# Three of 32 V stores issued as row scatters, with eight of their rows moved to the SyncE queue

## The chip, the cores and the metric

The kernel runs on one core of one Trainium2 chip. The metric is device time in microseconds (us) from one launch to its end; three runs of the kernel before gave 736.78, 735.42 and 736.70, with a median of 736.7 us. Engine names are those of the profile: PE multiplies matrices, DVE and ACT work on vectors, POOL is GpSimd, and SP is SyncE, which only issues transfers here. All transfers, whichever engine issues them, are carried out by the core's 16 DMA engines.

## The reference, cut to what matters

One decoding step of attention (32 heads, a cache of 8192 keys and values of width 128 for each head) is added to a gated MLP, and the function returns the output and the gradients of all its inputs.

```
q = (xn @ wq).reshape(B, 1, 32, 128)                  # xn: layernorm of x
p = softmax(einsum("bhqd,bhkd->bhqk", q, k_cache) * Dh**-0.5)
o = einsum("bhqk,bhkd->bhqd", p, v_cache)
out = x + o.reshape(B, 1, 4096) @ wo + swiglu(xn; w1, w3, w2)
outputs: out, d x, d k_cache, d v_cache, d wq, d wo, d w1, d w3, d w2
```

For each head the gradients of the two caches are outer products, d V = p x (d o) and d K = (d s) x q, as large as the caches: 2 MB of bf16 for each of K and V of each head. So the kernel reads 151 MB, writes 151 MB and computes little.

## The kernel before, in words

**Slots.** A head's K or V is one tile of 128 partitions x 8192 values: 16,384 bytes in each partition, 2 MB in all. There are ten such slots (kv0 to kv9). Four of them first hold the MLP's weights. A slot's life is: loaded with K or V of a head, read by PE, overwritten in place by DVE with the gradient (`outer`, L460 to L471, two instructions of half a tile), stored, loaded again. Ahead, V of head h is called Vh and its store likewise.

**Queues.** Every K and V load is issued by SP through `fifo` (L104), strictly in order: V0, K1, V1 and so on as slots come free. `store` (L473) issues the gradient's store from POOL, puts the slot back on the list and calls `load_next` (L120), which gives the next load to SP; that load waits for the store's landing. POOL also issues the stores of d wo (L505, 640 KB for a group of four heads) and d wq (L514, 640 KB), and the loads of a group's wq and wo (L111, L113). An instruction that waits holds up all that stands behind it on its engine; POOL and SP are such queues.

**Order.** The order of instructions is written out by hand (`manual_schedule`, L72). In `head(h)` (L729), DVE first finishes V of head h-1 (`outers_a`, whose `store("V", h-1)` issues Vh-1) and half of K, and in the middle of the head the rest of K (`outers_b`, store of K). In a head whose number is a multiple of four, `fin_wo` then issues d wo of the group before. So around V8 POOL's order is V7, K7, d wo, **V8**, K8, V9, d wq, K9, V10, K10; around V16 and V24 it is the same with 8 or 16 added. The MLP (L538) stands ahead of head 2.

**DMA waits.** DMAs take eight semaphores in turn on POOL and eight on SP, so each also waits for the landing of the one eight before it on its own engine. Besides that a store of V or K waits for DVE's outer product. No store waits for another store's data: their rows in DRAM are apart.

**A store as packets.** A store of a tile is 128 packets of 16,384 bytes, eight for each of the 16 DMA engines. Each engine adds one to the store's semaphore when its own eight have landed; the store has landed at the sixteenth.

## Time and profile before

| | |
|---|---|
| median of three runs | 736.7 us |
| the profiled execution's own time | 735.86 us |
| its span, first to last instruction | 734.1 us |
| transferred | 303.52 MB, mean 413 GB/s |
| busy share of the span: PE, DVE, ACT, POOL | 82%, 63%, 51%, 9% |
| store of a tile, issue to landing (median) | 45.2 us |
| load of K, of V, issue to landing (median) | 18.7, 22.3 us |
| one issue of a store on POOL, of a load on SP | 0.53, 0.33 us |

The page's part 1 gives busy times, part 2 the span in 40 slices with the DMA engines' busy share as one digit, part 3 the transfers by queue: q0 holds what POOL issues, q1 what SP issues, q8 and q14 are fetches of instructions. Part 6 gives, for each kind of transfer, its median time from issue to landing. Waits of SP's and POOL's queues have a view of their own, and the windows view gives the busy share of the DMA engines in chosen stretches: 1.00 is all sixteen, 0.06 is one of them.

### The profile page before, as it was taken

To read this page: it belongs to the slowest core of one execution; us is meant where nothing else is said; L and a number is where in the kernel's file an instruction comes from. 1 tells how busy PE (TensorE), PEld (TensorE's weight loads), DVE (VectorE), ACT (ScalarE), POOL (GpSimd) and SP (SyncE) were. 2 spreads that over 40 slices of the span, in tenths; PEclk is the share of its full clock that TensorE was granted. 3 is DMA by queue.
4 is the path that set the end of the run, shared out by engine and by line. 5 is a ranking of instruction groups with operands and counts; after the bars stand their busy time and mean duration, and the time that the engine had idled before them with its cause. 6 is when DMAs were issued, how large, how long until landed. Compare 5 with 4: busy or idle time off the path is not lost.

```text
span 734.1 us, 13013 instructions
## 1 busy us (share of the span) xinstructions
PE 601.6 (82%) x5186; PEld 374.7 (51%) x5193; DVE 460.3 (63%) x811; ACT 375.5 (51%) x727; POOL 64.7 (9%) x109
## 2 busy tenths in 40 slices
PE   4988589999899899988897869878798797886920
PEld 2556466665565566544554545544464454554510
DVE  4279637687867776767475555667367674664780
ACT  3641646655666666654454446544465453554500
POOL 0110100001011100200010100201002000001010
PEclk9996799999999999999899989999899998998955
DMA  8999999999999999999999999999999999999991
GB/s 351 402 413 419 426 425 419 430 429 430 427 429 421 427 426 427 423 427 425 428 429 413 427 427 423 422 428 428 428 427 413 427 426 429 428 420 430 423 410 79
DMA packets 27134, 303.52 MB, mean 413 GB/s; under 512 B 2798, under 2 KB 4146, under 8 KB 10434
## 3 DMA queue, kind: packets, MB, share of 16 engines
q0 software_dynamic: 14944, 160.52, 52.0%
q1 hardware_dynamic: 12126, 142.17, 46.0%
q8 instruction: 41, 0.67, 0.3%
q14 instruction: 19, 0.16, 0.1%
q10 hardware_dynamic: 4, 0.00, 0.0%
HBM read 151.34 MB, written 151.34 MB: 412 GB/s over the span
## 4 chain that ended last, share of the span: by engine, by line
DMA 30%; PE 28%; issue 17%; another core or an unknown queue 11%; DVE 7%; ACT 3%; POOL 1%; SPq 0%; POOLq 0%; ACTq 0%; DVEq 0%
DMA wo_g<-in_A_wo_dram 16%; PE pT L314 13%; DMA out_dram<-kv 8%; DMA kv<-in_A_k_cache_dram 4%; PE sA L335 4%; PE X L429 2%; PE dA L335 2%; DMA kv<-in_A_v_cache_dram 2%; DVE kv L462 2%; PE m L352 1%; ACT kv L624 1%; DVE side L253 1%; PE gu_ps L543 1%; PE dh_ps L554 1%
## 5 line engine op out<-in xcount | busy, mean ns | idle before, releaser
L316 ACT COPY KT<-pT 128x512 f32<-128x512 f32 x512 | 288.0, 588 | 231.0 <-PE pT L314 211.8
L314 PE MATMUL pT<-ident_f,kv 128*128 128x128 f32 x2048 | 304.6, 287 | 52.1 <-DMA kv<-in_A_k_cache_dram 34.5
L314 PEld LDWEIGHTS pT<-ident_f,kv 128*128 128x128 f32 x2048 | 234.2, 147 | 144.0 <-PE pT L314 52.1
L462 DVE TENSOR_TENSOR kv<-qd,U 128x4096 bf16<-128x4096 bf16 x64 | 146.0, 2283 | 0.0
L462 DVE TENSOR_TENSOR kv<-qd,P 128x4096 bf16<-128x4096 bf16 x64 | 143.6, 2284 | 0.0
L429 PE MATMUL X<-kv,Z 128*32 128x512 bf16 x1024 | 97.4, 414 | 1.4 <-DVE Z L446 1.4
L335 PE MATMUL dA<-KT,qz 128*32 128x512 bf16 x512 | 83.7, 406 | 0.0
L335 PE MATMUL sA<-KT,qz 128*32 128x512 bf16 x512 | 82.4, 401 | 0.0
L477 POOL DMA_DIRECT2D out_dram<-kv x64 | 34.7, 543 | 393.6 <-DVE kv L462 184.7
L412 DVE SCALAR_TENSOR_TENSOR U<-m,P 128x64 bf16<-128x64 f32 x32 | 7.4, 232 | 86.0 <-PE m L352 86.0
L429 PEld LDWEIGHTS <-Z 128*32 128x32 bf16 x1024 | 33.2, 101 | 35.1 <-issue 8.9
L335 PEld LDWEIGHTS <-qz 128*32 128x32 bf16 x1024 | 29.5, 95 | 40.4 <-issue 37.8
L378 DVE TENSOR_REDUCE mrow<-m 128x1 f32<-128x64 f32 x32 | 7.2, 224 | 56.1 <-PE m L352 56.0
L352 PE MATMUL m<-selc,KT 64*128 64x64 f32 x256 | 30.8, 244 | 11.7 <-ACT KT L342 11.7
L352 PEld LDWEIGHTS m<-selc,KT 64*128 64x128 f32 x256 | 21.8, 146 | 34.0 <-ACT KT L342 24.5
L253 DVE SCALAR_TENSOR_TENSOR side<-wo_g,g_bc 128x640 bf16<-128x640 bf16 x32 | 26.2, 820 | 16.6 <-DMA wo_g<-in_A_wo_dram 16.2
L372 ACT CAST qd<-pT 128x256 bf16<-128x256 f32 x32 | 11.9, 373 | 39.5 <-DVE kv L462 30.8
L385 DVE TENSOR_REDUCE negM<-m 128x1 f32<-128x128 f32 x32 | 9.3, 291 | 32.9 <-PE m L382 32.9
L510 DVE SCALAR_TENSOR_TENSOR wq_g<-wq_g,side 128x512 bf16<-128x512 bf16 x40 | 27.3, 682 | 0.0
L444 DVE SCALAR_TENSOR_TENSOR U<-m,P 128x128 bf16<-128x128 f32 x32 | 11.4, 356 | 15.4 <-PE m L442 15.4
L402 DVE RECIPROCAL rZ<-m 128x1 f32<-128x1 f32 x32 | 5.3, 166 | 24.2 <-PE m L396 24.2
L342 ACT COPY KT<-dA 64x512 f32<-64x512 f32 x32 | 18.6, 583 | 3.4 <-PE dA L335 3.4
(162 smaller groups left out, 392.1 us busy)
## 6 DMA issues: line engine op xcount, KB each, us to landing
out_dram<-kv POOLq DMA_DIRECT2D x64, 2048.0 KB, 45.2
kv<-in_A_k_cache_dram SPq DMA_DIRECT2D x32, 2048.0 KB, 18.7
kv<-in_A_v_cache_dram SPq DMA_DIRECT2D x32, 2048.0 KB, 22.3
out_dram<-wo_g POOLq DMA_DIRECT2D x8, 640.0 KB, 51.0
out_dram<-wq_g POOLq DMA_DIRECT2D x8, 640.0 KB, 48.6
wq_g<-in_A_wq_dram POOLq DMA_DIRECT2D x7, 640.0 KB, 30.8
wo_g<-in_A_wo_dram POOLq DMA_DIRECT2D x7, 640.0 KB, 34.9
kv<-in_B_w_dram SPq DMA_DIRECT2D x2, 1728.0 KB
```

Source lines behind the costliest of these rows:

```text
L253: nc.vector.scalar_tensor_tensor(junk[:], G_["wo"][:, hh, :], 1.0, g_bc[:], ALU.mult, ALU.mult, accum_out=G_["do"][:, hh:hh + 1])
L314: nc.tensor.transpose(pT[:, k * P:(k + 1) * P], W3[:, 4 * c + k, :], ident_f[:])
L316: nc.scalar.copy(KT[:].rearrange("p k w -> p (k w)"), pT[:])
L335: nc.tensor.matmul(S_[kind][q:q + QW, :], lhsT=S_["qz"][:, o:o + QW], rhs=KTb[c][:, par, :], start=(c0 == 0 and par == 0), stop=(c0 == NCH ...
L342: nc.scalar.copy(XS[0:QH].rearrange("p k w -> p (k w)"), S_.pop(kind)[0:QH, :])
L352: nc.tensor.matmul(S_["m"][:, b0:b0 + 4 * J].rearrange("p (x c k t) -> p k x c t", x=4, k=4, t=2)[:, k], lhsT=XS[0:QH, k, :], rhs=selc[0:Q ...
L372: nc.scalar.copy(qd[:].rearrange("p a d -> p (a d)"), hd[h].pop("ps_r"))
L429: nc.tensor.matmul(xg["X"][q:q + QW, :], lhsT=Z[:, o:o + QW], rhs=W[:, N4 * i:N4 * (i + 1)], start=(slot == 0 and i < 4), stop=(slot == NS ...
L444: nc.vector.scalar_tensor_tensor(S_["U2"][:], S_["V"][:, 0:J].unsqueeze(2).to_broadcast([P, J, 2]), S_["m"][:, OC + NS:OC + NS + 1], S_["P ...
L462: nc.vector.tensor_tensor(dst[:, lo * DH:hi * DH].rearrange("p (j a b) -> p j a b", a=DH // 2, b=2), vec.rearrange("p (a b) -> p a b", b=2 ...
L477: nc.gpsimd.dma_start((dkc if kind == "K" else dvc)[h], t[:])
L510: nc.vector.scalar_tensor_tensor(wq_g[:, ci, :], wq_g[:, ci, :], 1.0, dqb, ALU.mult, ALU.mult, accum_out=dxa[:, ci, g:g + 1])
```

## The change

For heads 8, 16 and 24 the V store is issued as an indirect DMA (a row scatter): a list of 128 row numbers says to which row of the output each partition's 16,384 bytes go. For partitions 16 to 19 and 48 to 51 the list holds a number beyond the bound (2 to the 20th is added), so that these eight rows are left out; SP then stores them in two transfers of four partitions each. The list is built once, at the start, by one iota on POOL and seven small instructions on DVE, from the identity matrix that is there already.

```
+    ROW_HEADS = (8, 16, 24)
+    SPARE = (16, 48)
+    dv_rows = out_3.rearrange("b h (p j) d -> (b h p) (j d)", p=P)
+    row_ix = consts.tile([P, 4], mybir.dt.uint32, name="row_ix")
+    row_i = consts.tile([P, 4], mybir.dt.int32, name="row_i")
+    nc.gpsimd.iota(row_i[:], [[8 * P, 4]], base=8 * P, channel_multiplier=1)
+    row_f = consts.tile([P, 4], F32, name="row_f")
+    nc.vector.tensor_copy(row_f[:], row_i[:])
+    skip = consts.tile([P, 2], F32, name="skip")
+    for n, lo in enumerate(SPARE):
+        nc.vector.tensor_reduce(skip[:, n:n + 1], ident_f[:, lo:lo + 4], AX.X, ALU.add)
+    nc.vector.tensor_tensor(skip[:, 0:1], skip[:, 0:1], skip[:, 1:2], ALU.add)
+    nc.vector.tensor_scalar(skip[:, 0:1], skip[:, 0:1], float(2 ** 20), None, ALU.mult)
+    nc.vector.tensor_scalar(row_f[:], row_f[:], skip[:, 0:1], None, ALU.add)
+    nc.vector.tensor_copy(row_ix[:], row_f[:])
...
-        nc.gpsimd.dma_start((dkc if kind == "K" else dvc)[h], t[:])
+        if kind == "V" and h in ROW_HEADS:
+            n = ROW_HEADS.index(h)
+            nc.gpsimd.indirect_dma_start(dv_rows, bass.IndirectOffsetOnAxis(ap=row_ix[:, n:n + 1], axis=0), t[:], None,
+                                         bounds_check=H * P - 1, oob_is_err=False)
+            for lo in SPARE:
+                fifo(dvc[h][lo:lo + 4], t[lo:lo + 4])
+        else:
+            nc.gpsimd.dma_start((dkc if kind == "K" else dvc)[h], t[:])
```

What the built program makes of it: a scatter's destination is the whole V output, since its rows are known only at run time. So the scatter of V8 waits for the landing of V7 (as well as for its outer product), V9 waits for the landing of the scatter, and so does SP's first four-row transfer; the load that takes the slot next waits for both four-row transfers. V16 and V24 wait in the same way. K8, which stands between V8 and V9 on POOL, has no such wait. Nothing else changes its place on any engine.

## The prediction

> **What bounds the kernel now.** I read the page's transfers first, then SP's waits, then the windows over the end of the span.

> ```profile
> span 734.1 us, 13013 instructions
> ...
> GB/s 351 402 413 419 426 425 419 430 429 430 427 429 421 427 426 427 423 427 425 428 429 413 427 427 423 422 428 428 428 427 413 427 426 429 428 420 430 423 410 79
> ...
> q0 software_dynamic: 14944, 160.52, 52.0%
> q1 hardware_dynamic: 12126, 142.17, 46.0%
> q8 instruction: 41, 0.67, 0.3%
> ```

> The rate is flat at 420 to 430 GB/s from the fourth slice to the last but two, and the queues' packets fill 98% of 16 engines' span: DMA is the bound, and no arithmetic engine is (PE 82%). The last slice falls to 79 GB/s. [...]

> ```profile
> SPq L105 <- DMA out_dram<-kv: 605.0, 58, 22.2
> ```

> SP waits 605 us for stores to land: a load starts when a store frees its slot, never for want of being asked. Now the end:

> ```profile
> 712.00:714.00 2.00, 0.56 (x2) 0.50 (x2) 1.22 (x8) 0.00 (x0) 0.87 (x1) 0.50 1.02 420
> ...
> 718.00:720.00 2.00, 0.00 (x0) 0.00 (x0) 0.00 (x0) 0.00 (x0) 0.00 (x0) 0.50 0.46 188
> 720.00:722.00 2.00, 0.00 (x0) 0.00 (x0) 0.00 (x0) 0.00 (x0) 0.00 (x0) 0.50 0.20 81
> 722.00:724.00 2.00, 0.00 (x0) 0.00 (x0) 0.00 (x0) 0.00 (x0) 0.00 (x0) 0.50 0.12 50
> 724.00:726.00 2.00, 0.00 (x0) 0.00 (x0) 0.00 (x0) 0.00 (x0) 0.00 (x0) 0.50 0.06 25
> 726.00:728.00 2.00, 0.00 (x0) 0.00 (x0) 0.00 (x0) 0.00 (x0) 0.00 (x0) 0.50 0.06 24
> 728.00:730.00 2.00, 0.00 (x0) 0.00 (x0) 0.00 (x0) 0.00 (x0) 0.00 (x0) 0.50 0.07 27
> 730.00:732.00 2.00, 0.00 (x0) 0.00 (x0) 0.00 (x0) 0.00 (x0) 0.00 (x0) 0.50 0.02 6
> ```

> The column before the last is the DMA engines' busy share. At 712 all sixteen work; by 722 two are left (0.12), and from 724 to 730 the share is 0.06, one sixteenth: **one DMA engine finishes alone, some 6.4 us after the fifteenth**. The sixteen increments of the last store's semaphore (d wq) say it more closely: half by 719.91, the fifteenth at 724.58, the sixteenth at 731.02. The lag grew: on V7's store the last was 0.7 us behind the fifteenth (248.38), on V16's 11.6 (444.41), on V24's 15.1 (617.19). Which engine it is the trace does not name. But the last q8 packet ends at 702.60, the next packet on that engine (it begins 15 ns before, as at other q8 packets) opens a gapless run of 71 packets, and that run is the one that ends last. [...]

> **The change, part by part.**

> *Removed.* Three scatters leave out 8 rows each: 24 packets of 16,384 bytes. Such a packet takes 611 ns, and the next on its engine starts 4 ns before its end: 24 x 0.607 = 14.6 us less for whatever engine had them. That all eight rows are one engine's share I cannot read in the trace. [...] Bounds for the late engine: all eight rows are its own, 14.6 us; four are, 7.3; none, 0. I take the first. Either of the first two ends it before the fifteenth, and then the fifteenth is the end: **gain 731.02 - 724.58 = 6.4 us**, not 14.6.

> *Added on other engines.* The eight rows go in six transfers of four rows. The only four-row transfer now is of fin_bf; its packets run on four engines which end all work at 716.5 to 719.7. If the new ones take the same four, each gains 6 x 0.607 = 3.6 us and ends by 723.4, before 724.58: cost 0.

> *First added wait: the scatter for the V store before it.* V8 was issued at 228.45 and may now go only when V7 has landed, 248.38: 20 us later. For V16 it is 391.13 to 422.92, for V24 562.88 to 595.69. Queued behind it on POOL stand K8, V9, d wq; none of them is needed by DVE or PE, only by SP, for slots. What matters is that no engine that sets the end runs out of packets. The late engine still holds K7 and d wo when V7 lands: they land at 254.72 and 261.21, so its cover is 12.8 us (12.8 at V16 and V24 too). Needed is the time from an issue to a first packet; the first POOL transfer, issued at 33.98, had its first packet at 38.23: 4.25 us. Engines that are ahead do run dry (the first is through d wo at 416.96, 6 us before V15's landing), but they have 5 to 15 us to spare at the end. Cost 0.

> *Second added wait: V9 for the scatter's landing.* In between stands K8 alone, and on the last engine it lands 6.5, 5.8 and 5.7 us after V8, V16 and V24 (276.48 - 269.99 and so on). Against 4.25 us this cover holds, though barely; on the fifteenth engine it is 4.8, 9.7 and 9.8. I take 0.2 us for each scatter. Bounds: 0, and 4.25 us a wait if there is no cover.

> *Third: SP.* The first four-row transfer waits for the scatter, the slot's load for both. The load was due at that same landing, so it comes later by two issues (0.66 us) and one small landing: 1.45 us by SP's small stores of KT at the idle end, 14 to 20 us by the loads that share a full queue. I take 4 us, as the queue in front of it has mostly drained (SP alone, issues at 254.85 and then 270.14). One slot of ten is late by that; stores wait 45.2 us in their queue, so it is hidden. If not, 3 x 4 = 12 us.

> *The scatter itself.* No row shows an indirect transfer. A direct store's issue is 0.53 us, the costliest on POOL 0.99 (wq, 640 descriptors); up to 8.5 us the first wait's cover hides it (12.8 - 4.25). Below zero is excluded, as it moves the same bytes. I take 1 us, hidden. Start: seven DVE instructions of 0.06 to 0.37 us (rows L164 to L184), about 1.2 us, before L231, which waited 5.57 us for ACT; iota lies beside POOL's 32.55 us idle. Cost 0.

> *Sum.* -6.4 + 3 x 0.2 = -5.8. The profiled execution took 735.86 (span 734.1 and 1.8 around it): 730.1. The median is 0.8 above it: 736.7 - 5.8 = **730.9 us**.

> **Rivals.**

> *A: relief on the wrong engine.* The scatter may deal out its rows otherwise than a plain store, or the late engine may be another. For: the trace names no engine; it rules out only four, those of fin_bf's packets. Against: no row. The end is then the late engine's, which was covered at each wait: 736.7 + 3 x 0.2 = 737.3. [...]

> *B: the store queue runs dry, slower than before.* One mechanism: after a landing POOL needs longer to feed the queue than the packets behind it last, so all engines are left with loads at most, and loads wait for stores. Place: the second wait, and the first if an indirect issue is long. It decides from 5.7 us after the scatter's landing, or 12.8 after the V store's. For: V8 was issued 41.5 us ahead of its landing, now some 21 (269.99 - 248.38), and the loads behind SP's wait stop too: from 246 to 252 no load packet is in flight even now. Against: 4.25 us. Price with the cover gone: two waits x 4.25 x 3 = 25 us; with half of it filled by loads 13; on top of A or of the forecast: 736.7 + 13 - 6.4 = 743 to 762, most likely 746.

> *C: the other engines gain too.* If the late engine holds back the loads of all, its relief could let the fifteenth end sooner, towards the median's 719.91: 736.7 - 11 = 726. Against: all 16 are busy to 713, so nobody waits for it. Small.

> **How the numbers follow.** Forecast 0.47, A 0.20, B 0.29, C 0.04. No row decides between the forecast and A; that they stand at seven to three is a judgement, and B's chance is what the thin covers of 5.7 us and the unseen scatter leave open. The predicted time is the forecast's, 730.9. The range goes from 727.5 (half of C; the forecast less its 0.6 and a spread of 1) to 742 (over all of A and the edge of B, the hidden prices partly showing); outside lie most of B and some of C, 2 in 10. The forecast alone is 729 to 733. A measurement can tell about 0.2%, 1.5 us, from no change: faster is the forecast and C, 0.51; A is mostly within it, 0.14; slower is B and the rest of A, 0.35.

> **What would show it.** Right: the windows at the end have no stretch of 6 us at 0.06; the sixteenth increment of the last store follows the fifteenth within 2 us; the share stays near 1.00 after each scatter. A: that stretch is there as before. B: the share drops below 0.9 for some us around 250, 272, 425, 445, 597 and 620, and GB/s dips in those slices; SP's longest wait grows well over 22.2 us. I would be wrong above all if scattered rows are not dealt out like a plain store's, or if their descriptors take POOL many us.

## The result, and the profile after

The changed kernel takes **749.25 us** (median of four runs, 749.17 to 749.64); the kernel before, on the same chip, 736.24 (735.42 to 736.78). The ratio is 1.0179, with a 95% interval of 1.0161 to 1.0196: slower by 13 us, where 5.8 us less had been forecast. The time lies outside the range.

The page of the changed kernel answers to the lines shown of before:

```profile
span 747.4 us, 13037 instructions
...
GB/s 347 400 414 413 427 430 410 420 427 428 430 426 417 422 382 394 413 426 427 428 428 420 379 410 374 411 414 431 427 424 417 423 322 377 398 427 425 427 433 197
...
q0 software_dynamic: 14944, 160.13, 51.6%
q1 hardware_dynamic: 12174, 142.56, 46.3%
q8 instruction: 41, 0.67, 0.3%
```

q0 has lost 0.39 MB and q1 gained it: 24 packets of 16,384 bytes went from POOL's queue to SP's, so the change does what it says. The rate, flat before, has three dips: slices 15 and 16 (382, 394), 23 and 25 (379, 374), 33 to 35 (322, 377, 398). One slice is 18.7 us, so these are the stretches after V8, V16 and V24. They are the loss; now the end, in the windows view (the DMA engines' share is the column before the last):

```profile
712.00:714.00 2.00, 1.05 (x16) 0.34 (x16) 1.97 (x3) 0.53 (x1) 0.00 (x0) 1.00 1.05 449
...
734.00:736.00 2.00, 0.00 (x0) 0.00 (x0) 0.00 (x0) 0.00 (x0) 0.00 (x0) 0.50 0.91 367
736.00:738.00 2.00, 0.00 (x0) 0.00 (x0) 0.00 (x0) 0.00 (x0) 0.00 (x0) 0.50 0.40 166
738.00:740.00 2.00, 0.00 (x0) 0.00 (x0) 0.00 (x0) 0.00 (x0) 0.00 (x0) 0.50 0.28 113
740.00:742.00 2.00, 0.00 (x0) 0.00 (x0) 0.00 (x0) 0.00 (x0) 0.00 (x0) 0.50 0.17 70
742.00:744.00 2.00, 0.00 (x0) 0.00 (x0) 0.00 (x0) 0.00 (x0) 0.00 (x0) 0.50 0.12 49
744.00:746.00 2.00, 0.00 (x0) 0.00 (x0) 0.00 (x0) 0.00 (x0) 0.00 (x0) 0.50 0.00 0
```

The lone engine of before is gone: no stretch stays at 0.06, and on the last store's semaphore the sixteenth increment follows the fifteenth by 0.1 us (6.4 before). But a group has taken its place. The sixteen increments end at 744.44, and counted back from there lie at 0, 0.1, 2.3, 4.1 and 4.3 us, then, after a gap, eleven at 7.4 to 8.9. **Five engines are late together.** At the landing of 275.60 all sixteen were still within 5.0 us; at that of 305.27 five are within 3.7 and eleven are 9.9 to 13.8 ahead. The group comes into being right after the first scatter.

POOL's and SP's timelines around V8 (start, duration, instruction, and in brackets the idle time before it with what ended it):

```profile
250.01 1.04 POOL L495 DMA_INDIRECT out_dram<-kv,row_ix  x1 [25.19 <-DMA out_dram<-kv]
251.05 0.57 POOL L500 DMA_DIRECT2D out_dram<-kv  x1
271.27 0.53 POOL L500 DMA_DIRECT2D out_dram<-kv  x1 [19.65 <-DVE side L269]
```

```profile
255.47 0.33 SPq L105 DMA_DIRECT2D kv<-in_A_v_cache_dram  x1
270.80 2.41 SPq L105 DMA_DIRECT2D out_dram<-kv  x2
284.25 0.37 SPq L105 DMA_DIRECT2D kv<-in_A_k_cache_dram  x1
```

The scatter goes at 250.01 instead of 228.45, V9 at 271.27 (the scatter has just landed; the name in the bracket is not the cause), and SP's next load comes 13.5 us after the two four-row transfers. In the trace's packets of that stretch, those of the four-row transfers last, in order of start:

```
271.57 3.29   272.04 3.29   272.66 3.45   272.76 2.44
277.73 1.76   278.46 4.01   278.82 3.90   278.91 2.85
```

Each was forecast at 0.61 us. Beside them runs a chain of POOL's packets, each starting as the one before ends: 272.68, 273.89, 275.11, then 277.75, 278.99, 280.20, and each of them takes 1.21 to 1.26 us instead of 0.61. So five engines are slow at once, the four that carry the rows and one more. I call the last one **the owner**: the engine whose plain stores take the rows of partitions 16 to 19 and 48 to 51. V16 and V24 look the same (four-row packets up to 4.43 and 4.65 us). That a single engine has all eight rows, the packets show: those that the scatter of V8 leaves out stand as eight packets of 4 bytes, 9 ns each, in one engine's queue between its d wo and its K8, from 261.95 to 265.04 us; it is the same at V16 (438.81 to 441.90) and V24 (611.60 to 615.01), and each time that engine is the last to land d wo (261.8, 438.7 and 610.4 us).

The waits bite too. Windows of 4 us:

```profile
424.00:428.00 4.00, 4.00 (x37) 2.36 (x30) 4.00 (x3) 2.15 (x4) 0.00 (x0) 1.00 0.79 275
...
446.00:450.00 4.00, 3.86 (x32) 2.60 (x33) 3.05 (x2) 2.59 (x7) 2.50 (x5) 1.00 0.90 373
...
602.00:606.00 4.00, 4.00 (x41) 2.39 (x40) 3.98 (x3) 1.88 (x4) 0.19 (x1) 1.00 0.35 141
```

Before V16's and V24's scatter the share falls to 0.79 and 0.35, after V16's to 0.90. From the packets' times around the three scatters, some 100 engine-us are idle, 6 us on each engine; before there were none. The 0.35 ahead of V24's scatter is five to six engines of sixteen.

### The profile page after: what moved, and what is told of

The parts are those of the page before. It is cut to its first block, busy times and chain, and to the rows that moved or that the text cites. A ratio compares the mean times of both kernels' runs of the same rounds, so it can differ in the third digit from the quotient of the medians.

```text
span 747.4 us, 13037 instructions
## 1 busy us (share of the span) xinstructions
PE 598.0 (80%) x5186; PEld 374.1 (50%) x5193; DVE 461.3 (62%) x818; ACT 375.4 (50%) x727; POOL 68.6 (9%) x110
## 3 DMA queue, kind: packets, MB, share of 16 engines
q0 software_dynamic: 14944, 160.13, 51.6%
## 4 chain that ended last, share of the span: by engine, by line
PE 40%; DMA 29%; DVE 9%; another core or an unknown queue 8%; issue 7%; ACT 4%; POOL 1%; SPq 0%; ACTq 0%; POOLq 0%; DVEq 0%
PE pT L330 19%; DMA out_dram<-kv 18%; DMA kv<-in_A_k_cache_dram 10%; PE sA L351 6%; DVE kv L478 4%; PE dA L351 4%; PE X L445 4%; PE m L368 2%; ACT KT L332 2%; DMA wo_g<-in_A_wo_dram 2%; ACT kv L647 1%; PE gu_ps L566 1%; DVE side L269 1%; PE dh_ps L577 1%
## 5 line engine op out<-in xcount | busy, mean ns | idle before, releaser
L445 PE MATMUL X<-kv,Z 128*32 128x512 bf16 x1024 | 95.8, 409 | 1.7 <-DVE Z L462 1.7
L358 ACT COPY KT<-dA 64x512 f32<-64x512 f32 x32 | 18.7, 583 | 3.1 <-PE dA L351 3.1
```

Of the source, the lines that this page charges most:

```text
L358: nc.scalar.copy(XS[0:QH].rearrange("p k w -> p (k w)"), S_.pop(kind)[0:QH, :])
L445: nc.tensor.matmul(xg["X"][q:q + QW, :], lhsT=Z[:, o:o + QW], rhs=W[:, N4 * i:N4 * (i + 1)], start=(slot == 0 and i < 4), stop=(slot == NS ...
```

## The experiments

By port I mean no more than what neighbouring rows share in these times. The probe of idle transfers below (`e9_rows_alone`) speaks for it: a packet takes 0.61 us for four rows four apart, 2.14 to 2.32 for partitions 16 to 19 and 1.14 to 1.24 for four rows thirty-two apart, the time of two that share. Partitions 48 to 51 are not in it; in the change the second four packets, theirs by the order of issue, take 1.76 to 4.01 us, and the owner's beside them 1.22 to 1.26.

### Waits, relief and readers taken apart

Three of the next four kernels make, with the change itself, a table of two by two. The first, `e1_all_rows`, keeps the waits alone:

```
-    nc.vector.tensor_scalar(skip[:, 0:1], skip[:, 0:1], float(2 ** 20), None, ALU.mult)
+    nc.vector.tensor_scalar(skip[:, 0:1], skip[:, 0:1], 0.0, None, ALU.mult)
...
-            for lo in SPARE:
-                fifo(dvc[h][lo:lo + 4], t[lo:lo + 4])
```

> The three V stores (heads 8, 16, 24) are row scatters of all 128 rows, and there are no four-row transfers: the waits of the scatter for the V store before it, and of the V store after it for the scatter, are there alone, with no relief of an engine and no readers from elsewhere. Theory port (the four-row transfers read four partitions behind one SBUF port, with four DMA engines and the owner at once, and four engines lose some 7 us at each scatter; the waits then find these engines late): no group of five engines lags after a scatter, no packet lasts over 1.5 us around it, the waits cost little, 737 to 741 us with the lone engine at the end as before. Theory waits (POOL's and SP's waits run the queues dry by themselves): 745 to 750 us, DMA share below 0.9 around each scatter as in the changed kernel. Theory form (four-row transfers are slow wherever their rows lie): as theory port here.

Measured: 740.64 us, ratio 1.0063 (1.0046 to 1.0079). No group of five lags. The waits alone cost 4.4 us, not 13:

```profile
270.00:274.00 4.00, 3.77 (x44) 2.32 (x40) 1.51 (x5) 2.55 (x6) 2.99 (x5) 1.00 1.01 344
...
424.00:428.00 4.00, 4.00 (x32) 2.56 (x31) 4.00 (x3) 2.15 (x4) 1.54 (x1) 0.98 0.75 236
446.00:450.00 4.00, 3.82 (x32) 2.47 (x31) 1.57 (x2) 3.01 (x6) 2.98 (x5) 1.00 0.83 246
```

The share falls, and in the first of these lines it is full and the rate still only 344 GB/s: SP's loads start anew after the stop, and from 40 to 705 us 85 of their packets take over 1.15 us (4 before), 84 of them in six bursts, each a few us long, one behind each of the six waits. Waits have a second price, in the packets that follow. It comes with the restart and not with loads being alone: in `e13_beside_loads` below, where nearly everything is loads, the packets of the first 2 us take up to 1.7 us and none that starts after 4.3 us takes over 0.63.

`e2_left_out` has waits and relief (the two `fifo` lines are gone, the eight rows stay left out):

> The scatters leave out partitions 16-19 and 48-51, and nothing stores these rows: eight rows each of V's outputs of heads 8, 16 and 24 are not written. Waits and relief without the four-row transfers. Theory port: no lagging group; if the eight rows belong to the late engine, it ends with the fifteenth and the time is 731 to 735 us; if they belong to another, 737 to 740 and the stretch of 0.06 at the end stays. Theory waits: 743 to 750 us. Theory form: as theory port.

Measured: 736.8 us (732.0 to 739.8 in ten runs), ratio 1.0004 (0.9982 to 1.0027); the time lies between the two ranges that were expected (731 to 735 and 737 to 740). The sixteenth increment follows the fifteenth by 0.8 us: the eight rows do belong to the late engine, and rival A of the prediction falls. Against `e1_all_rows` the relief brings 3.8 us; the waits give back what it brings.

`e3_side` has relief and readers without POOL's waits:

```
-    dv_rows = out_3.rearrange("b h (p j) d -> (b h p) (j d)", p=P)
+    dv_rows = nc.dram_tensor("side_rows", [H * P, KVN], BF16, kind="Internal").ap()
+    side_four = nc.dram_tensor("side_four", [3, 2, 4, KVN], BF16, kind="Internal").ap()
...
-                fifo(dvc[h][lo:lo + 4], t[lo:lo + 4])
+                fifo(side_four[n, k], t[lo:lo + 4])
```

> The scatters and the four-row transfers write to DRAM tensors beside the outputs, so that no V store waits for a scatter and no scatter for a V store; the V outputs of heads 8, 16 and 24 are not written. SP's waits for the slot stay. Relief and four-row transfers without POOL's waits. Theory port: four-row packets still last 2 to 4.6 us, five engines lag by some 7 us more after each scatter, and with no wait to run dry in the time is 737 to 745 us. Theory waits: no loss, 729 to 733 us as forecast. Theory form: as theory port.

Measured: 738.75 us, ratio 1.0031 (1.0017 to 1.0046). After V8 the four-row packets last 2.35 to 3.67 us, the owner's 1.20 to 1.24, and five engines lag (at the landing of 337.48: 0 to 4.5 us, the others 8.6 to 16.8). No engine is idle around the three scatters:

```profile
424.00:428.00 4.00, 4.00 (x27) 2.38 (x22) 4.00 (x3) 1.09 (x3) 0.53 (x1) 0.72 1.02 430
446.00:450.00 4.00, 4.00 (x43) 2.63 (x40) 4.00 (x2) 2.37 (x5) 0.00 (x0) 1.00 1.07 391
```

In the second window all engines are busy (1.07) at 391 GB/s: the loss is inside the packets. This is the line for theory waits to explain, and it can't. What I call the readers includes what the four-row transfers hold up on SP: its next load goes at 281.62 us, in `e5_relief` below at 266.46. As no engine is idle, that delay by itself doesn't show in the time here.

`e5_relief` (as `e3_side`, without the `fifo` lines) is the relief alone:

> The scatters write to a DRAM tensor beside the outputs and there are no four-row transfers; the V outputs of heads 8, 16 and 24 are not written. So neither POOL's added waits nor the added readers are there: the forecast's relief alone. Theory port: the lone engine at the end is gone, 729 to 732 us (the forecast's 730.9 less its three waits is 730.3); with e2 (relief and waits), e3 (relief and readers) and the changed kernel this makes a table of two by two, in which waits and readers together cost more than their sum. Theory waits: the same here. Rival A of the prediction (relief on the wrong engine): 736 to 738 us, the stretch of 0.06 at the end stays.

Measured: 731.89 us (728.2 to 734.7 in ten runs), ratio 0.9939 (0.9913 to 0.9964). The end has no lone engine (0.8 us between the last two):

```profile
720.00:722.00 2.00, 0.00 (x0) 0.00 (x0) 0.00 (x0) 0.00 (x0) 0.00 (x0) 0.50 0.28 113
722.00:724.00 2.00, 0.00 (x0) 0.00 (x0) 0.00 (x0) 0.00 (x0) 0.00 (x0) 0.50 0.12 48
724.00:726.00 2.00, 0.00 (x0) 0.00 (x0) 0.00 (x0) 0.00 (x0) 0.00 (x0) 0.50 0.00 0
```

| all with the relief | without POOL's waits | with POOL's waits |
|---|---|---|
| eight rows stored by nobody | 731.89 (`e5_relief`) | 736.8 (`e2_left_out`) |
| eight rows in four-row transfers | 738.75 (`e3_side`) | 749.25 (the change) |

Waits alone add 4.9 us, readers alone 6.9, both 17.4: 5.6 more than their sum (the cells with ten runs spread over 6 to 8 us, so each difference of medians is good to some 2 us, and the excess to some 3). The link is in the trace: a wait ends at the landing on the last engine, the readers make five engines late, and the other eleven, done early, run dry until then. Around the three scatters some 40 engine-us are idle in `e2_left_out` and some 100 in the change; the 60 more are 3.7 us on each engine, most of the 5.6. What makes up the rest, SP's later loads among others, no run separates.

### The form of the transfer

`e4_spread` takes other rows, four partitions apart (`lo:lo + 16:4` instead of `lo:lo + 4`, in the list and in the transfers):

> As the changed kernel, but the rows left out and moved by SyncE are partitions 16, 20, 24, 28 and 48, 52, 56, 60: again eight rows in two transfers of four, whose rows lie four partitions apart instead of side by side. All waits stay. Theory port: each row has a port whose owner alone shares it, four-row packets last 0.6 to 1.3 us, no group of five lags by 7 us, 736 to 742 us (the relief falls on four engines, two rows each, so the lone engine stays late unless it is one of them). Theory form: packets still 2.4 to 4.6 us, 746 to 750 us. Theory waits: 745 to 750 us whatever the packets last.

Measured: 739.2 us, ratio 1.0032 (1.0018 to 1.0047), 10 us less than the change, with the same bytes, waits and number of transfers. Of the packets of V8's rows, none lasts over 1.54 us (0.61 to 1.54, then 0.69 to 1.22). Theory form would have kept 2.4 to 4.6, theory waits 745 to 750 us: both fall. That the relief goes to four engines, two rows each, is an assumption of the expectation that no run here tests.

`e8_single` moves the eight rows in eight transfers of one row:

```
-                fifo(dvc[h][lo:lo + 4], t[lo:lo + 4])
+                for r in range(lo, lo + 4):
+                    fifo(dvc[h][r:r + 1], t[r:r + 1])
```

> As the changed kernel, but SyncE moves the eight rows in eight transfers of one row each instead of two of four: one reader at a time beside the owner of the port, all waits and the whole relief kept. Theory port: a single row's packet takes at most 1.3 us (sharing with the owner alone), no five engines lag, 735 to 741 us, near the 736.8 of the kernel whose eight rows nothing stores. Theory form (any small transfer from these rows is slow): packets of 2.4 us and more, 746 us or more. What could spoil it: eight rows in a line on one engine take 8 to 10 us of it at each scatter, so that this engine is the last one.

Measured: 745.39 us, ratio 1.0108 (1.0079 to 1.0138). The packets are short, 0.61 to 1.24 us, as theory port says, but the time is not: what the expectation named as the spoiler came. The time alone lies nearer to theory form's 746 than to theory port's 735 to 741; the packets are what decides here. On the last store fourteen increments lie 6.8 to 7.3 us ahead of the last, and the fifteenth 1.3: two engines are late. That these are the one that carries the single rows and the owner is a reading; the trace names no engine.

### The port by itself

`e9_rows_alone` runs the transfers one after the other on an idle chip (one run, which goes through them twice):

> No part of the computation: the disputed transfers one after the other on an idle chip, each waiting for the one before it: one row of 16,384 bytes, two rows side by side, four side by side (partitions 16 to 19), four rows four apart, four rows thirty-two apart, eight side by side, a load into four rows; then a plain store of 128 rows and scatters of 128 and of 120 rows. Theory port: packets of the one row and of the rows four or thirty-two apart take about 0.6 us, of two side by side about 1, of four side by side 2 us (four readers share what one port gives); eight side by side as four. Theory form: four rows take the same wherever they lie. The outputs are not written.

SP's timeline (each transfer waits for the landing of the one before, so the step to the next line is its time; L67 is one row, L68 two side by side, L69 four side by side, L70 four rows four apart, L71 four rows thirty-two apart):

```profile
5.25 0.30 SPq L67 DMA_DIRECT2D side<-rows  x1
6.94 0.22 SPq L68 DMA_DIRECT2D side<-rows  x1
9.28 0.24 SPq L69 DMA_DIRECT2D side<-rows  x1
12.92 0.67 SPq L70 DMA_DIRECT2D side<-rows  x1
15.25 0.48 SPq L71 DMA_DIRECT2D side<-rows  x1
18.02 0.27 SPq L72 DMA_DIRECT2D side<-rows  x1
```

The four side by side take 3.64 us, the four apart 2.33, of which 0.67 is the issue. The packets: one row 0.614 us; two side by side 1.23 and 1.24; four side by side 2.14 to 2.32; four apart 0.614 each; thirty-two apart 1.14 to 1.24, not the 0.6 that was expected but the time of two side by side (partitions 0, 32, 64 and 96; which of them share, the times don't tell); eight side by side 2.14 to 2.49. All stores of four rows write the same four rows of DRAM, so the destination is not what makes the difference. A load into four rows side by side takes 1.18 to 1.35 us a packet the first time and 0.72 to 1.42 the second, less than the store from them. The time of the stores is that of the readers of one port, 16,384 bytes in about 0.6 us or 27 GB/s for the port, which is also what one engine moves alone. In these stores a port has nothing over for a second engine.

`e10_rows_beside` and `e13_beside_loads` put such transfers beside a stream of plain stores and a stream of loads:

> No part of the computation: first sixteen plain stores of 128 rows in a row, and beside them on SyncE, one after the other and twice over, one row, four rows four apart, and four rows side by side (partitions 16 to 19); then nine loads of 128 rows in a row with the same three row transfers beside them once. The outputs are not written. It asks what the owner of the port pays, and whether it pays when it loads. Theory port: beside stores, one row and the rows four apart take about 1.2 us and so do the owner's packets; the four side by side take 3 us each or more, and the owner's packets in that time 1.2 us or more, so that it loses about half a packet for each row that is moved off it (0.6 us for each of the first kind). Beside loads the rows read a port that nobody else reads: one row 0.6 us, four side by side 2.3 us as on the idle chip, and the owner loses nothing. Theory form: the owner's packets stay at 0.61 us throughout.

All nine row transfers ran beside the stores, so the half about loads went to the second kernel. Beside stores one row takes 0.61 us, not 1.2; four apart 0.61 to 1.06; four side by side 0.61 to 3.88. The owner loses: during the last four rows (58.73 to 63.1 us) its five packets from 58.00 on take 1.09, 1.21, 1.22, 1.25 and 0.73 us, 2.4 us more than five of 0.611. That is 0.61 us for each row moved off it, which is what the row would have cost on it. **In this probe the relief is given back in full.**

> No part of the computation: eleven loads of 128 rows in a row, and beside them on SyncE, one after the other and twice over, one row, four rows four apart and four rows side by side (partitions 16 to 19) stored from the first tile loaded. No plain store runs, so the owner of the port only writes into SBUF. The kernel of the same transfers beside stores showed the owner losing about 0.6 us for each row that others read (its packets 1.21 instead of 0.61 us while they read). Theory port, if reads alone share: one row 0.6 us, four side by side 2.3 us as on the idle chip, and no load packet of the owner slowed beyond what other loads show. Theory port, if reads and writes share: the owner's load packets go to 1.2 us during the row transfers and the four side by side take 3 us or more. Theory form: the four side by side take 0.6 us.

Beside loads the four side by side take 0.61 to 0.75 us, less than the 2.14 to 2.32 of the idle chip and the figure that the expectation gave to theory form; it is `e4_spread` and `e9_rows_alone` that speak against that theory. No load packet that starts after 4.3 us takes over 0.63. So stores that read one port hinder each other, and loads, which write there, neither suffer nor harm, as far as packet times tell. Why the rows are even faster there than on the idle chip stays open; they begin 3.8 us after their issue, on the idle chip 0.7.

### The two waits apart

In `e11_first_wait` the stores of V9, V17 and V25, in `e12_second_wait` those of V7, V15 and V23 go to another tensor, all else as in `e1_all_rows` (`beside` is a new DRAM tensor; the second kernel has `h + 1` where the first has `h - 1`):

```
+        elif kind == "V" and h - 1 in ROW_HEADS:
+            nc.gpsimd.dma_start(beside[ROW_HEADS.index(h - 1)], t[:])
```

> As the kernel that scatters all 128 rows and has no four-row transfers (740.64 us), but the V stores of heads 9, 17 and 25 go to a DRAM tensor beside the outputs (these heads of that output are not written), so that they don't wait for the scatter: the scatter's own wait for the V store before it is left alone. Theory waits as the trace of that kernel shows it (41 of its 66 idle engine-us lie ahead of the scatters): 738.5 to 740 us. The prediction's step (first wait costs nothing, since the late engine has 12.8 us of cover): 736 to 737.

> The other half: the V stores of heads 7, 15 and 23 go to a DRAM tensor beside the outputs (these heads of that output are not written), so that the scatter finds no store to wait for, or only one that landed long before; heads 9, 17 and 25 still wait for the scatter. From the idle time behind the scatters (25 of 66 engine-us): 737.5 to 739 us. The prediction's step (0.2 us for each): 736.8.

Measured: 737.15 us for the first wait alone, ratio 1.0007 (0.9998 to 1.0017), and 739.51 for the second, 1.0044 (1.0028 to 1.0060). POOL's timeline of the second kernel shows it at V9:

```profile
228.70 2.83 POOL L496 DMA_INDIRECT out_dram<-kv,row_ix  x1 [6.19 <-DVE kv L479]
237.79 0.57 POOL L501 DMA_DIRECT2D out_dram<-kv  x1 [6.26 <-DVE kv L479]
270.53 0.53 POOL L501 DMA_DIRECT2D out_dram<-kv  x1 [32.17 <-DMA out_dram<-kv,row_ix]
```

The two sum to 3.3 of the 4.4 us, and the second is most of it. My expectation, from where the idle time lay, had them the other way round. The first alone is not clear of zero. But `e11_first_wait` is not quite the first wait alone. The scatter's destination is the whole V output, so V10, the next V store that goes there, waits for it too:

```profile
251.27 0.53 POOL L499 DMA_DIRECT2D beside<-kv  x1
251.80 0.88 POOL L538 DMA_DIRECT2D out_dram<-wq_g  x1
254.90 0.55 POOL L501 DMA_DIRECT2D out_dram<-kv  x1 [2.22 <-DVE kv L479]
271.03 0.53 POOL L501 DMA_DIRECT2D out_dram<-kv  x1 [15.57 <-issue]
```

V10 goes at 271.03, when the scatter has landed (270.49). By then K8, V9, d wq and K9 stand in the queue behind the scatter instead of K8 alone, and practically no engine is idle behind the three scatters (under 1 engine-us; nearly 100 in `e12_second_wait`, some 30 in `e1_all_rows`). So it is not the wait for the scatter as such that costs, but how little is queued behind it. On the last store the sixteenth increment comes at 731.29 us in `e11_first_wait` and at 733.98 in `e12_second_wait` (731.02 before), so only the wait with K8 alone behind the scatter delays the last engine. A reading of it, which no run tests: ahead of the scatter those engines idle that are early anyway; behind it the store queue is all but empty everywhere (in `e1_all_rows` 1 of 16 engines carries a packet of POOL's queue from 448 to 451 us), and what restarts there is slow for all.

### Attempts at a faster version

`e6_first` scatters head 0 alone, with single rows:

> Only the first V store (head 0) is a scatter that leaves out the eight rows, and SyncE moves them in eight transfers of one row; heads 8, 16 and 24 are plain stores. No V store stands before it, so one wait of the two is left, and the queue is still short when it comes. Relief of one engine by 8 x 0.607 = 4.9 us of the 6.4 that it is behind at the end. Theory port: 731 to 735 us, faster than both kernels. Theory waits: a start that runs dry for 5 to 15 us, 737 to 745.

Measured: 737.57 us, ratio 1.0017 (1.0005 to 1.0028). The expectation of theory port was 731 to 735. At the end the last two engines are 0.1 us apart and 6.5 us behind the next: nothing is gained. That they are the one with the single rows and the owner, as in `e8_single`, is a reading.

If rows cost nothing beside loads, they might go behind a load instead of ahead of it: in `e14_rows_later` `store` keeps the scattered slot back, sends its rows after the next load, and frees it one store later; `e15_one_head` does so for head 8 alone (`ROW_HEADS = (8,)`).

```
+            held.append([t, h, 0])
+            return
...
+        if held:
+            held[0][2] += 1
+            t, h, n = held[0]
+            if n == 1:
+                for lo in SPARE:
+                    fifo(dvc[h][lo:lo + 4], t[lo:lo + 4])
+            else:
+                held.pop()
+                free_slots.append(t)
+                load_next()
```

> As the changed kernel, the whole computation, but SyncE sends the two four-row transfers only after the load of the next slot that comes free, and the slot of the scattered head is refilled after a further one, so that SP's loads don't stand behind the rows. The rows then run beside loads and stores in turn instead of beside stores alone. Theory port with reads alone sharing (beside loads a four-row packet took 0.61 us and no load packet was slowed; beside stores 2.4 to 4.6 us): four-row packets 0.6 to 2 us, the owner gives back little, five engines lag by less than 4 us at a scatter, 736 to 742 us (736.8 is the kernel whose eight rows nothing stores). If the place in the queue doesn't matter: packets of 2.4 us and more, 746 to 750 us.

> The same order, but only the V store of head 8 is a scatter; heads 16 and 24 are plain stores. Relief of 8 x 0.607 = 4.9 us of the 6.4 that the lone engine is behind, a third of the waits' price of 4.4 us (1.5), and of the readers' what the order leaves. Theory port with reads alone sharing: 732 to 736 us, faster than both kernels by up to 4 us. If the relief is given back to the readers: 737 to 740 us.

Measured: 759.45 us, ratio 1.0315 (1.0300 to 1.0331), above both expected ranges, and 736.45 us, 1.0001 (0.9988 to 1.0013), between the two. In `e14_rows_later` the order is as meant:

```profile
273.45 0.33 SPq L105 DMA_DIRECT2D kv<-in_A_k_cache_dram  x1
274.27 1.86 SPq L105 DMA_DIRECT2D out_dram<-kv  x2
280.94 0.37 SPq L105 DMA_DIRECT2D kv<-in_A_v_cache_dram  x1
```

But seven of the eight four-row packets after V8, from 288.68 us on, take 3.2 to 5.9 us, and after V16 they take up to 8.4, longer than before; the owner's stores after V16 take 1.8. So the step from "free beside loads alone" to "cheap between loads and stores" is wrong. Why a mixed stream is worse for the readers than stores alone stays open; no run here separates it. No version beat the kernel before.

## Why the prediction was wrong, step by step

- **What bounds the kernel, and the late engine**: right, but for the run behind the last q8 packet. With the eight rows left out the lone engine is gone (0.8 us between the last two in `e5_relief` and `e2_left_out`), so it is the owner of their port, and rival A is out. The run of 71 packets is not that engine's: followed from 702.59 us with eight packets and a semaphore's write of 4 bytes to each store of a tile, the engine behind the last q8 packet of the kernel before has its last packet at 719.5 us, while the late one's is at 730.6. In the change, too, the q8 packet of 260.37 to 261.37 us is on another engine than the rows left out, which writes d wo's semaphore at 261.33. Why the late engine is late, no run shows.
- **Removed, gain 6.4 us**: that all eight rows are one engine's, the term of 14.6 us, was a choice among three bounds, and the change's eight packets of 4 bytes on one engine bear it out. The sign is right, the size 4.3 us where nobody reads the rows (736.13 to 731.89; by the interval of the ratio 2.7 to 6.4). In the change itself it doesn't stay: 17 packets of the owner at some 1.22 us around the three scatters give back at least 17 x 0.61 = 10.4 of the 14.6 us.
- **Added on other engines, 3.6 us on each of four, cost 0**: this is the step that failed. The term was packets times 0.607, as if only the engine that carries a packet mattered. V8's eight packets sum to 25.0 us, 6.2 on each engine where 1.2 was forecast. Readers alone cost 6.9 us (`e3_side` against `e5_relief`), beside the waits 12.5 (the change against `e2_left_out`).
- **First wait, 0**: right within the noise, 0.5 us for three (737.15 against the 736.69 of the kernel before in that comparison, ratio 0.9998 to 1.0017); the 12.8 us of cover hold.
- **Second wait, 0.2 us each**: too small. It costs 2.8 us for three, 0.9 each, inside the bounds of 0 and 4.25. The cover of 5.7 us, K8 alone, was too thin: with three stores more behind the scatter (`e11_first_wait`) the same wait costs next to nothing.
- **SP, 4 us late and hidden**: late by 12.2 to 13.5 us. Where POOL doesn't wait it was hidden: in `e3_side` the load comes at 281.62 us, in `e5_relief` at 266.46, and no engine is idle in either. In the change, where the store queue runs low at the same time, no run separates it.
- **The scatter itself, 1 us, hidden**: its issue took 1.04, 2.51 and 1.7 us. `e11_first_wait` contains it, and wait and issue together cost the 0.5 us above.
- **Sum and rivals**: rival B, with 746, named the right sign, and the queues do run dry. But its mechanism alone is worth 4.4 us (`e1_all_rows`), not 13. The time comes from a mechanism that no rival held, readers of one port, and from what it does to B's waits.

Of the three signs that I had named for the forecast, two (no stretch at 0.06, increments within 2 us) came out while the time went the other way: they tell that one engine was relieved or overtaken, not that the end came sooner. The third, a share near 1.00 after each scatter, did not: it is 0.90 from 446 to 450 us and 0.35 just ahead of V24's scatter.

## What to carry to other kernels

Work taken off a late DMA engine was a gain in one run alone, where nobody stored its rows and no store waited (4.3 us, `e5_relief`); four other engines that stored them at the same time took up to 4.65 us a packet instead of 0.61 and slowed the late engine's own to some 1.22. So price a transfer by the partitions that it reads at the same time as its neighbours, not by bytes and engines alone; on the idle chip a packet of four rows side by side took 2.14 to 2.32 us where one of four rows four apart took 0.61 (`e9_rows_alone`). And price waits and late engines together: a wait on a landing lasts until the latest engine's part has landed, and where waits alone cost 4.9 us and readers alone 6.9, both cost 17.4.

## What the runs showed of the hardware that was not expected

- A stored packet of 16,384 bytes takes 0.61 us for one row, 1.23 for two side by side, 2.14 to 2.32 for four (`e9_rows_alone`); beside plain stores four side by side take 0.61 to 3.88 us (`e10_rows_beside`), beside loads alone 0.61 to 0.75 (`e13_beside_loads`), beside loads and stores together 3.2 to 8.4 (`e14_rows_later`).
- When loads start anew after a stop, the engines are all busy at 344 GB/s for some us (`e1_all_rows`, 270 to 274 us), where the kernel before has up to 430 in a slice; in a stream of loads that goes on, their packets take 0.61 to 0.63 us (`e13_beside_loads`).
- An indirect store's issue on POOL takes 1.00 and 1.02 us on the idle chip (`e9_rows_alone`) and up to 2.85 in the kernel (`e6_first`); a plain one's of a tile 0.53 to 0.71.
